# Attention by feature maps, then a cosine layer: queries in one wide step, key maxima as two float32r parts, a new order

## The chip, the cores and the metric

The kernel runs on one core of one Trainium2 chip. The core has TensorE (PE, matrix products into PSUM banks), VectorE (DVE), ScalarE (ACT), GpSimd (POOL) and SyncE (SP, which issues the DMAs). The metric is the time of one execution on the device, in microseconds (us). Line numbers (L574 and the like) are lines of the kernel before.

## The reference

```
phi(x):  proj = x @ w_phi                              # (576, 64) @ (64, 128)
         proj = proj - max(abs(proj), axis=-1)
         return concat(exp(proj), exp(-proj))          # 256 features
q_p, k_p = phi(q), phi(k)
kv  = k_p.T @ v ;  z = sum of k_p over the tokens
out = (q_p @ kv) / (q_p @ z + 1e-6)                    # per batch and head
x   = out, heads side by side                          # (4608, 512)
h   = x @ w_in ;  g = h * cos(h) ;  result = g @ w_out # w_in (512, 2048), w_out (2048, 512)
```

q, k and v have 8 batches, 8 heads, 576 tokens and 64 columns, in float32. w_in and w_out are float64; the kernel gets their bits.

## The kernel before, in words

**Attention.** Two heads of a batch form a pair; there are 32 pairs (`attention(u)`). The two heads lie one above the other, 64 partitions each, so that two products with 64 rows run beside each other in PE's array. For the queries of a pair `q_mm` projects a half of the tokens, 288 columns, for both heads into two banks; `q_copy` brings each of the four results to SBUF on ACT, `q_red` reduces each on DVE to the greatest absolute value, `q_max` joins them, `q_spread` (POOL) copies them to all quarters of the partitions, `q_turn` (DVE) turns them back to the layout of the queries, `q_sub` (POOL, one for each head) subtracts and `exp_q` (ACT) makes both exponentials. For the keys `k_mm` projects four blocks of 128 tokens of each head with the tokens on the partitions and `k_end` the remaining 64 of both heads; `k_max` (DVE) takes the greatest absolute value of each token. In pairs 0 to 7 (`K_SUMS`) the subtraction is made by PE: `k_sub` adds the product of `minus` (a matrix with -1 on the diagonal) with the maxima, read 128 times over, into the same bank; in the other pairs DVE subtracts (L569). `exp_k` makes the exponentials, `kv_mm` the sums over tokens, `kv_out` copies them, `z_mm` and `n_mm` make denominator and numerator, `invert`, `spread`, `turn` and `times` the quotient.

**FFN.** Weights are turned from float64 bits into two float32r parts (`convert`, 16 slices, four of them partly on POOL). Nine chunks of 512 tokens are worked through in slices of 128 columns of w_in: `mm1` is 12 products, then ACT and DVE make h cos(h) and its two parts, and `mm2` (or four `one`) is 12 products.

**Order.** Every piece of work is a `Step` on an engine, numbered as it is made. `ORDER` is a written list of these numbers; each engine issues its steps in that order and waits at each for what it needs. `plan()` gives each PSUM bank to the next use in that order. The cost beside each `Step` is a number for the planner that made the list and has no part in the program that runs. A step with `port=True` reads and writes SBUF alone on DVE or POOL. A step takes its buffers (`take`) and the last user frees them.

Of the kernel before, what the change touches and what calls it, by code (L numbers as in the profile page):

```python
# [17 lines left out]
P = 128  # L18
TWO_PI = 6.283185307179586
PI_2 = 1.5707963267948966  # L20
CT = 512
# [4 lines left out]
def phi_attention_then_cos_ffn(ctx: ExitStack, tc: tile.TileContext, qT, kT, vS, vT, w_phi, w_in, w_out, out):  # L26
# [41 lines left out]
    class Step:  # L68
# [16 lines left out]
    SHAPE = dict(mm1="full", mm2="full", one="full", k_mm="upper", k_end="full", t_mm="upper", t_end="full", s_mm="full", k_sub="full", kv_mm="left", n_mm="left", z_mm="quarter", q_mm="upper")  # L85
    ORDER = [
# [196 lines left out]
    for j in range(2):  # L283
# [5 lines left out]
    DVE.memset(warm, 0.0)  # L289

    minus = const.tile([P, P], F32, name="minus")
    POOL.memset(minus, -1.0)
    POOL.affine_select(out=minus, in_=minus, pattern=[[-1, P]], compare_op=ALU.is_equal, fill=0.0, base=0,
                       channel_multiplier=1)

# [637 lines left out]
```

## Time and profile before

| | |
|---|---|
| median of 3 runs | 1083.51 us (1080.97 to 1084.04) |
| profiled execution | 1081.44 us, its span 1079.7 us |
| granted TensorE clock | 1.000 |
| PE, busy in the span | 1069.3 us, 7678 products |
| DVE | 711.8 us, 1203 instructions |
| ACT | 720.8 us, 1388 instructions |
| POOL | 157.6 us, 187 instructions |
| DMA | 160.72 MB, mean 149 GB/s |

The span runs from the first to the last instruction of the profiled execution. A float32 product stands as two records of PE, a float32r product as one. Products overlap, so the time that one costs in a row of them is the distance from start to start. "Idle before" and what stands behind an arrow say how long an engine stood before an instruction and what it waited for.

### The profile page before, as it was taken

To read this page: it belongs to the slowest core of one execution; us is meant where nothing else is said; L and a number is where in the kernel's file an instruction comes from. 1 tells how busy PE (TensorE), PEld (TensorE's weight loads), DVE (VectorE), ACT (ScalarE), POOL (GpSimd) and SP (SyncE) were. 2 spreads that over 40 slices of the span, in tenths; PEclk is the share of its full clock that TensorE was granted. 3 is DMA by queue.
4 is the path that set the end of the run, shared out by engine and by line. 5 is a ranking of instruction groups with operands and counts; after the bars stand their busy time and mean duration, and the time that the engine had idled before them with its cause. 6 is when DMAs were issued, how large, how long until landed. Compare 5 with 4: busy or idle time off the path is not lost.

```text
span 1079.7 us, 19604 instructions
## 1 busy us (share of the span) xinstructions
PE 1069.3 (99%) x7678; PEld 830.6 (77%) x7678; DVE 711.8 (66%) x1203; ACT 720.8 (67%) x1388; POOL 157.6 (15%) x187
## 2 busy tenths in 40 slices
PE   9999999999999999999999999999999999999998
PEld 6666677787888887788677787786877878888886
DVE  6899999988898877645667456764564353434333
ACT  7888898878666669754785766757556654544443
POOL 5664322000000310101121011120120000000000
PEclk9999999999999999999999999999999999999999
DMA  7535644667655544275242643163231720540541
GB/s 217 154 119 189 180 132 143 209 202 249 235 167 191 210 153 153 105 242 185 63 123 73 243 148 107 56 232 135 75 87 47 277 90 1 187 174 10 185 157 49
DMA packets 92604, 160.72 MB, mean 149 GB/s; under 512 B 43744, under 2 KB 52064, under 8 KB 84320
## 3 DMA queue, kind: packets, MB, share of 16 engines
q1 hardware_dynamic: 92352, 159.41, 44.3%
q8 instruction: 60, 0.98, 0.4%
q14 instruction: 32, 0.26, 0.1%
q10 hardware_dynamic: 160, 0.07, 0.0%
HBM read 117.51 MB, written 41.94 MB: 148 GB/s over the span
## 4 chain that ended last, share of the span: by engine, by line
PE 87%; DVE 5%; issue 0%; DMA 0%; POOL 0%; ACT 0%; DVEq 0%; POOLq 0%
PE bank L782 36%; PE bank L816 12%; PE bank L818 12%; PE bank L817 12%; PE bank L675 4%; PE bank L626 4%; PE bank L665 2%; PE bank L434 2%; PE bank L476 2%; PE bank L632 1%; PE bank L552 1%; DMA out<-o_last 0%; DVE g_c__1300 L793 0%; DVE g_c__1130 L800 0%; DVE m_u__1584 L445 0%
## 5 line engine op out<-in xcount | busy, mean ns | idle before, releaser
L797 ACT ACT_TABLE_LOAD x23 | 29.5, 1283 | 0.4
L459 POOL COPY m_u__4056<-m_u__4056 32x36 f32<-32x36 f32 x3 | 1.6, 540 | 174.4 <-DVE m_u__4056 L454 174.3
L582 ACT ACT_TABLE_LOAD x15 | 19.2, 1283 | 0.8 <-DVE pk_u__2466 L569 0.5
L856 DVE TENSOR_TENSOR o<-bank,o 128x512 f32<-128x512 f32 x24 | 16.1, 678 | 0.1
L863 ACT ACTIVATE o<-bank 128x512 f32<-128x512 f32 x16 | 9.5, 592 | 5.5 <-PE bank L818 5.5
L782 PE MATMUL bank<-xh_c__6319,w 128*128 128x512 f32 x32 | 12.9, 402 | 0.0
L865 DVE COPY o<-bank 128x512 f32<-128x512 f32 x16 | 10.8, 674 | 3.1 <-PE bank L818 3.1
L782 PE MATMUL bank<-xh_c__5560,w 128*128 128x512 f32 x32 | 12.7, 398 | 0.0
L782 PE MATMUL bank<-xh_c__7588,w 128*128 128x512 f32 x32 | 12.7, 396 | 0.0
L782 PE MATMUL bank<-xh_c__4428,w 128*128 128x512 f32 x32 | 12.6, 393 | 0.0
L782 PE MATMUL bank<-xh_c__6921,w 128*128 128x512 f32 x32 | 12.5, 391 | 0.0
L782 PE MATMUL bank<-xh_c__6769,w 128*128 128x512 f32 x32 | 12.5, 390 | 0.0
L782 PE MATMUL bank<-xh_c__5807,w 128*128 128x512 f32 x32 | 12.5, 390 | 0.0
L782 PE MATMUL bank<-xh_c__7130,w 128*128 128x512 f32 x32 | 12.5, 390 | 0.0
L782 PE MATMUL bank<-xh_c__5878,w 128*128 128x512 f32 x32 | 12.5, 390 | 0.0
L782 PE MATMUL bank<-xh_c__7977,w 128*128 128x512 f32 x32 | 12.5, 390 | 0.0
L782 PE MATMUL bank<-xh_c__5928,w 128*128 128x512 f32 x32 | 12.5, 390 | 0.0
L782 PE MATMUL bank<-xh_c__8059,w 128*128 128x512 f32 x32 | 12.5, 390 | 0.0
L782 PE MATMUL bank<-xh_c__4632,w 128*128 128x512 f32 x32 | 12.5, 389 | 0.0
L782 PE MATMUL bank<-xh_c__8100,w 128*128 128x512 f32 x32 | 12.5, 389 | 0.0
L782 PE MATMUL bank<-xh_c__4557,w 128*128 128x512 f32 x32 | 12.5, 389 | 0.0
L782 PE MATMUL bank<-xh_c__4759,w 128*128 128x512 f32 x32 | 12.4, 389 | 0.0
(3872 smaller groups left out, 4075.7 us busy)
## 6 DMA issues: line engine op xcount, KB each, us to landing
w<-w_parts SPq DMA_DIRECT2D x48, 1024.0 KB, 5.3
w_parts<-w SPq DMA_DIRECT2D x16, 1024.0 KB, 5.7
vmain<-vS SPq DMA_DIRECT2D x32, 256.0 KB, 3.9
out<-o SPq DMA_DIRECT2D x32, 256.0 KB, 3.5
sums<-o SPq DMA_DIRECT2D x24, 256.0 KB, 3.3
o<-sums SPq DMA_DIRECT2D x24, 256.0 KB, 3.2
vtail<-vT SPq DMA_DIRECT2D x64, 16.0 KB, 3.4
out<-o_last SPq DMA_DIRECT2D x4, 256.0 KB, 2.0
```

What stands on the lines that cost most here:

```text
L434: PE.matmul(out=ps[j], lhsT=wphi[r, :], rhs=d["qr"][r, hf * HALF:(hf + 1) * HALF], start=True, stop=True)
L476: PE.matmul(out=ps[j][:, P * s:P * s + P], lhsT=x[r, P * s:P * s + P], rhs=wphi[r, :], start=(s == 0), stop=w, skip_group_check=True)
L582: ACT.activation(out=e[:, :, s * P:(s + 1) * P], in_=pk, func=AF.Exp, scale=1.0 - 2.0 * s)
L626: PE.matmul(out=acc[c:c + 64, n, i, :], lhsT=e[:, s, P * n + c:P * n + c + 64], rhs=vmain[u % 2][:, s, i, :], start=(s == 0 and i == 0 and ...
L665: PE.matmul(out=ps[32 * g:32 * g + 32], lhsT=d["z"][:, 2 * n + j, :], rhs=d["eq", j][:, n, hf * HALF:(hf + 1) * HALF], start=(n == 0), sto ...
L675: PE.matmul(out=d["nps", hf][64 * j:64 * j + 64], lhsT=d["kv"][:, 2 * n + j, :], rhs=d["eq", j][:, n, cut[hf]], start=(n == 0 and hf == 0) ...
L782: PE.matmul(out=h, lhsT=a[:, cs], rhs=d[b, kt], start=(k == 0), stop=(k == 3 * KT - 1))
L797: ACT.activation(out=m["g"], in_=m["g"], func=AF.Sin, bias=halfpi, scale=1.0)
L816: PE.matmul(out=a, lhsT=gh[:, t], rhs=w[:, 0], start=first, stop=False)
L817: PE.matmul(out=a, lhsT=gh[:, t], rhs=w[:, 1], start=False, stop=False)
L818: PE.matmul(out=a, lhsT=gl[:, t], rhs=w[:, 0], start=False, stop=last)
L856: DVE.tensor_tensor(out=o, in0=bank(acc[tb]), in1=o, op=ALU.add)
```

## The change

Queries: `q_mm` now projects 512 tokens of both heads in one step (two products with 512 columns), and a new step `q_end` projects the last 64 of both heads in one product with 128 columns over all 128 rows, from a block that is laid out on the host as the keys' already is. ACT copies two results of 512 columns and one of both ends; `q_red` reduces 576 columns of a head in one instruction. Keys of pairs 0 to 7: DVE splits each maximum into a float32r number and the float32r rest (`k_parts`, two instructions), and `k_sub` adds two float32r products in place of one in float32; `minus` is rounded to float32r once. `ORDER` is a new list, of 2848 steps instead of 2920. Code that no pair used (`Q_SUMS`, `t_mm`, `t_max`, `s_mm`, `s_exp`) is gone.

```diff
-    minus = const.tile([P, P], F32, name="minus")
+    minus_f = const.tile([P, P], F32, name="minus_f")
...
+    minus = const.tile([P, P], F32R, name="minus")
+    hi_of(POOL, minus, minus_f)
...
-            d["qr"] = new("qr", [P, S + P], F32, f"qr_u{u}_")
+            d["qr"] = new("qr", [P, (NSLOT + 1) * P], F32, f"qr_u{u}_")
-            SP.dma_start(out=d["qr"][:, 0:S + P if u in Q_SUMS else S], in_=qT[u][:, 0:S + P if u in Q_SUMS else S])
+            SP.dma_start(out=d["qr"], in_=qT[u])
...
-        def q_mm(hf):
+        def q_mm():
             for j in range(2):
                 r = slice(64 * j, 64 * j + 64)
-                PE.matmul(out=ps[j], lhsT=wphi[r, :], rhs=d["qr"][r, hf * HALF:(hf + 1) * HALF], start=True, stop=True)
+                PE.matmul(out=bank(qb[j]), lhsT=wphi[r, :], rhs=d["qr"][r, 0:CT], start=True, stop=True)
+        def q_end():
+            PE.matmul(out=bank(qb[2])[:, 0:P], lhsT=wphi, rhs=d["qr"][:, CT:CT + P], start=True, stop=True)
...
+            if i < 2:
+                ACT.activation(out=pq[:, i, 0:CT], in_=bank(qb[i]), func=AF.Copy, scale=1.0)
+            else:
+                ACT.activation(out=pq[:, :, CT:S], in_=bank(qb[2])[:, 0:P].rearrange("p (j s) -> p j s", j=2), func=AF.Copy,
+                               scale=1.0)
+        def q_red(j):
+            DVE.tensor_reduce(out=d["m1"][:, 2 * j * NJ:2 * (j + 1) * NJ],
+                              in_=d["pq"][:, j * S:(j + 1) * S].rearrange("p (j t) -> p j t", t=32), axis=AX.X,
                               op=ALU.max, apply_absolute_value=True, apply_transpose=True)
...
+        mm = Step("PE", 0.86, q_mm, [ld], take=qb[:2] + [b["pq"]], use=[b["qr"]], kind=phase + "q_mm")
+        me = Step("PE", 0.14, q_end, [ld], take=qb[2:], use=[b["qr"]], kind=phase + "q_end")
...
+        reds = [Step("DVE", 0.66, lambda j=j: q_red(j), [cps[j], cps[2]], use=[b["pq"]], kind=phase + "q_red")
+                for j in range(2)]
...
+        def k_parts(i):
+            tag = "pk" if i < 2 else "pk_t"
+            m = d["mk", i]
+            p = d["mp", i] = new(tag, [P, 2, NSLOT if i < 2 else 1], F32R, f"mp_u{u}_", "mp" + tag)
+            hi_of(DVE, p[:, 0], m)
+            lo_of(DVE, p[:, 1], m, p[:, 0])
         def k_sub(i):
...
-            PE.matmul(out=pv, lhsT=minus, rhs=d["mk", i].unsqueeze(2).broadcast_to([P, n, P]), start=False, stop=True,
-                      skip_group_check=True)
+            for r in range(2):
+                PE.matmul(out=pv, lhsT=minus, rhs=d["mp", i][:, r].unsqueeze(2).broadcast_to([P, n, P]), start=False,
+                          stop=(r == 1), skip_group_check=True)
...
-                kms[i] = Step("PE", 0.86 if i < 2 else 0.22, lambda i=i: k_sub(i), [kms[i]], use=[kb[i], pks[i]], kind="a.k_sub")
+                kms[i] = Step("DVE", 0.24, lambda i=i: k_parts(i), [kms[i]], use=[pks[i]], port=True, kind="a.k_parts")
+                kms[i] = Step("PE", 0.46 if i < 2 else 0.14, lambda i=i: k_sub(i), [kms[i]], use=[kb[i], pks[i]], kind="a.k_sub")
```

More of the change, by code (lines that the diff above doesn't have):

```diff
@@ L84, in phi_attention_then_cos_ffn @@
     SWITCH = dict(e=1.3, s=1.3, full=0.23, left=0.147, quarter=0.138, upper=0.195)
-    SHAPE = dict(mm1="full", mm2="full", one="full", k_mm="upper", k_end="full", t_mm="upper", t_end="full", s_mm="full", k_sub="full", kv_mm="left", n_mm="left", z_mm="quarter", q_mm="upper")
+    SHAPE = dict(mm1="full", mm2="full", one="full", k_mm="upper", k_end="full", q_end="full", k_sub="full", kv_mm="left", n_mm="left", z_mm="quarter", q_mm="upper")
     ORDER = [
[152 rows of a table removed]
[148 rows of a table added]
     ]
@@ L289, in phi_attention_then_cos_ffn @@
     DVE.memset(warm, 0.0)
-    minus = const.tile([P, P], F32, name="minus")
-    POOL.memset(minus, -1.0)
-    POOL.affine_select(out=minus, in_=minus, pattern=[[-1, P]], compare_op=ALU.is_equal, fill=0.0, base=0,
+    minus_f = const.tile([P, P], F32, name="minus_f")
+    POOL.memset(minus_f, -1.0)
+    POOL.affine_select(out=minus_f, in_=minus_f, pattern=[[-1, P]], compare_op=ALU.is_equal, fill=0.0, base=0,
                        channel_multiplier=1)
+    minus = const.tile([P, P], F32R, name="minus")
+    hi_of(POOL, minus, minus_f)
     vmain = [const.tile([P, NSLOT, 2, 65], F32, name=f"vmain{i}") for i in range(2)]
@@ L309, in phi_attention_then_cos_ffn @@
     Q_DVE = range(0)
-    Q_SUMS = range(0)
     K_SUMS = range(8)
@@ L427, in attention, with q_copy @@
         chain_v[u] = lv
-        def q_mm(hf):
-            d["qps", hf] = ps = [bank(d["qb", hf, j])[:, 0:HALF] for j in range(2)]
+        def q_mm():
             for j in range(2):
                 r = slice(64 * j, 64 * j + 64)
-                PE.matmul(out=ps[j], lhsT=wphi[r, :], rhs=d["qr"][r, hf * HALF:(hf + 1) * HALF], start=True, stop=True)
-        def q_copy(hf, j):
-            if (hf, j) == (0, 0):
+                PE.matmul(out=bank(qb[j]), lhsT=wphi[r, :], rhs=d["qr"][r, 0:CT], start=True, stop=True)
+        def q_end():
+            PE.matmul(out=bank(qb[2])[:, 0:P], lhsT=wphi, rhs=d["qr"][:, CT:CT + P], start=True, stop=True)
+        def q_copy(i):
+            if i == 0:
                 d["m1"] = new("pq", [P, 4 * NJ], F32, f"m1_u{u}_", "m1")
                 d["pq"] = new("pq", [P, 2 * S], F32, f"pq_u{u}_")
-            c = slice(j * S + hf * HALF, j * S + (hf + 1) * HALF)
-            ACT.activation(out=d["pq"][:, c], in_=d["qps", hf][j], func=AF.Copy, scale=1.0)
-        def q_red(hf, j):
-            c = slice(j * S + hf * HALF, j * S + (hf + 1) * HALF)
-            DVE.tensor_reduce(out=d["m1"][:, (2 * j + hf) * NJ:(2 * j + hf + 1) * NJ],
-                              in_=d["pq"][:, c].rearrange("p (j t) -> p j t", t=32), axis=AX.X,
+            pq = d["pq"].rearrange("p (j s) -> p j s", j=2)
+            if i < 2:
[6 more added lines that the diff above has]
+                              in_=d["pq"][:, j * S:(j + 1) * S].rearrange("p (j t) -> p j t", t=32), axis=AX.X,
                               op=ALU.max, apply_absolute_value=True, apply_transpose=True)
@@ L477, in project @@
                               start=(s == 0), stop=w, skip_group_check=True)
-        def t_mm():
-            project([bank(qb[j]) for j in range(2)], d["qr"], True)
-        def t_end():
-            PE.matmul(out=bank(qb[2])[:, 0:P], lhsT=d["qr"][:, S:S + P], rhs=wphi, start=True, stop=True)
-        def t_max(i):
-            n = NSLOT if i < 2 else 1
-            if i == 0:
-                d["mq"] = new("pq", [P, 4 * NJ], F32, f"m1_u{u}_", "m1")
-            DVE.tensor_reduce(out=d["mq"][:, NSLOT * i:NSLOT * i + n],
-                              in_=bank(qb[i])[:, 0:P * n].rearrange("p (g f) -> p g f", f=P), axis=AX.X, op=ALU.max,
-                              apply_absolute_value=True)
@@ L493, in s_mm @@
-        def s_mm():
-            ps = [bank(sb_[i]) for i in range(3)]
-            for j in range(2):
-                r = slice(64 * j, 64 * j + 64)
-                PE.matmul(out=ps[j], lhsT=wphi[r, :], rhs=d["qr"][r, 0:CT], start=True, stop=False, skip_group_check=True)
-            PE.matmul(out=ps[2][:, 0:P], lhsT=wphi, rhs=d["qr"][:, S:S + P], start=True, stop=False, skip_group_check=True)
-            for i in range(3):
-                n = NSLOT if i < 2 else 1
-                for s in range(n):
-                    c = NSLOT * i + s
-                    PE.matmul(out=ps[i][:, P * s:P * s + P], lhsT=d["mq"][:, c:c + 1].broadcast_to([P, P]), rhs=minus,
-                              start=False, stop=True, skip_group_check=True)
@@ L506, in s_exp @@
-        def s_exp(j):
-            e = d["eq", j] = new("eq", [P, 2, S], F32, f"eq_u{u}_")
-            for s in range(2):
-                ACT.activation(out=e[:, s, 0:CT], in_=bank(sb_[j]), func=AF.Exp, scale=1.0 - 2.0 * s)
-            for s in range(2):
-                ACT.activation(out=e[:, s, CT:S], in_=bank(sb_[2])[:, 64 * j:64 * j + 64], func=AF.Exp, scale=1.0 - 2.0 * s)
-        eqs, eqb = [], []
-        if u in Q_SUMS:
-            qb = [Buf("bank", "a") for _ in range(3)]
-            sb_ = [Buf("bank", "a") for _ in range(3)]
-            tm = Step("PE", 0.88, t_mm, [ld], take=qb[:2] + [b["pq"]], use=[b["qr"]], kind="a.t_mm")
-            te = Step("PE", 0.22, t_end, [ld], take=qb[2:], use=[b["qr"]], kind="a.t_end")
-            tr = None
-            reds = []
-            for i in range(3):
-                tr = Step("DVE", 0.67 if i < 2 else 0.28, lambda i=i: t_max(i), [te if i == 2 else tm, tr], use=[qb[i], b["pq"]],
-                          kind="a.t_max")
-                reds.append(tr)
-            sm = Step("PE", 3.4, s_mm, reds, take=sb_, use=[b["qr"], b["pq"]], kind="a.s_mm")
-            qs = [sm]
-        else:
-            reds, mm = [], None
-            for hf in range(2):
-                pair = [Buf("bank", "a"), Buf("bank", "a")]
-                d["qb", hf, 0], d["qb", hf, 1] = pair
-                mm = Step("PE", 0.49, lambda hf=hf: q_mm(hf), [ld, mm], take=pair + ([] if hf else [b["pq"]]),
-                          use=[b["qr"]] + ([b["pq"]] if hf else []), kind=phase + "q_mm")
-                for j in range(2):
-                    cp = Step("ACT", 0.3, lambda hf=hf, j=j: q_copy(hf, j), [mm] + reds[:1], use=[pair[j], b["pq"]],
-                              kind=phase + "q_copy")
-                    reds.append(cp)
-            cps, reds = reds, []
-            for i, cp in enumerate(cps):
-                reds.append(Step("DVE", 0.37, lambda i=i: q_red(i // 2, i % 2), [cp], use=[b["pq"]], kind=phase + "q_red"))
-            qm = Step("DVE", 0.41, q_max, reds, take=[b["bq"]], use=[b["pq"]], port=True, kind=phase + "q_max")
-            qm = Step("POOL", 0.45, q_spread, [qm], use=[b["bq"]], port=True, kind=phase + "q_spread")
-            qm = Step("DVE", 1.3, q_turn, [qm], use=[b["bq"]], kind=phase + "q_turn")
-            qs = [Step(qname, qcost, lambda j=j: q_sub(j), [qm], use=[b["pq"], b["bq"]], port=True, kind=phase + "q_sub") for j in range(2)]
@@ new lines, in attention @@
+        eqs, eqb = [], []
+        qb = [Buf("bank", "a") for _ in range(3)]
+        mm = Step("PE", 0.86, q_mm, [ld], take=qb[:2] + [b["pq"]], use=[b["qr"]], kind=phase + "q_mm")
+        me = Step("PE", 0.14, q_end, [ld], take=qb[2:], use=[b["qr"]], kind=phase + "q_end")
+        cps = []
+        for i in range(3):
+            cps.append(Step("ACT", 0.52 if i < 2 else 0.2, lambda i=i: q_copy(i), [me if i == 2 else mm] + cps[:1], use=[qb[i], b["pq"]],
+                            kind=phase + "q_copy"))
@@ new lines, in attention @@
+        reds = [Step("DVE", 0.66, lambda j=j: q_red(j), [cps[j], cps[2]], use=[b["pq"]], kind=phase + "q_red")
+                for j in range(2)]
+        qm = Step("DVE", 0.41, q_max, reds, take=[b["bq"]], use=[b["pq"]], port=True, kind=phase + "q_max")
+        qm = Step("POOL", 0.45, q_spread, [qm], use=[b["bq"]], port=True, kind=phase + "q_spread")
+        qm = Step("DVE", 1.3, q_turn, [qm], use=[b["bq"]], kind=phase + "q_turn")
+        qs = [Step(qname, qcost, lambda j=j: q_sub(j), [qm], use=[b["pq"], b["bq"]], port=True, kind=phase + "q_sub") for j in range(2)]
@@ L564, in k_max @@
             DVE.tensor_reduce(out=m, in_=pv, axis=AX.X, op=ALU.max, apply_absolute_value=True)
-            d["mk", i] = m
             if u in K_SUMS:
+                d["mk", i] = m
                 return
@@ L600, in attention @@
             if u in K_SUMS:
-                kms[i] = Step("PE", 0.86 if i < 2 else 0.22, lambda i=i: k_sub(i), [kms[i]], use=[kb[i], pks[i]], kind="a.k_sub")
-        gate = [] if early or u in Q_SUMS or u in K_SUMS else kms + qs
+                kms[i] = Step("DVE", 0.24, lambda i=i: k_parts(i), [kms[i]], use=[pks[i]], port=True, kind="a.k_parts")
+                kms[i] = Step("PE", 0.46 if i < 2 else 0.14, lambda i=i: k_sub(i), [kms[i]], use=[kb[i], pks[i]], kind="a.k_sub")
+        gate = [] if early or u in K_SUMS else kms + qs
         eks, ekb = [], []
@@ L610, in attention @@
             e = Buf("eq")
-            eqs.append(Step("ACT", 1.15 if u not in Q_SUMS else 1.75, lambda j=j: (s_exp if u in Q_SUMS else exp_q)(j),
-                            ([sm] if u in Q_SUMS else [qs[j]]) + gate, take=[e], use=[sb_[j], sb_[2]] if u in Q_SUMS else [b["pq"]],
+            eqs.append(Step("ACT", 1.15, lambda j=j: exp_q(j),
+                            [qs[j]] + gate, take=[e], use=[b["pq"]],
                             table="e", kind=phase + "exp_q"))
@@ L898, in _arrange, with blocks @@
     m = S - n * P
-    def blocks(x, w):
+    def blocks(x):
+        w = n * P
         xp = x.reshape(NU, 2, S, D).transpose(0, 1, 3, 2)
@@ L908, in blocks @@
         return xT.reshape(NU, 2 * D, w + P)
-    qT, kT = blocks(q, S), blocks(k, n * P)
+    qT, kT = blocks(q), blocks(k)
     vp = v.reshape(NU, 2, S, D)
```

300 rows, old and new, of the table ORDER are left out of this document.

## The prediction

> **What bounds the kernel now.** I read the page's engine shares first, then the busy time by stages, then what TensorE (PE) waited for, and then the timeline of PE and VectorE (DVE) in the first 110 us, where all steps of the change on keys lie.
>
> ```profile
> span 1079.7 us, 19604 instructions
> ...
> PE 1069.3 (99%) x7678; PEld 830.6 (77%) x7678; DVE 711.8 (66%) x1203; ACT 720.8 (67%) x1388; POOL 157.6 (15%) x187
> ```
>
> ```profile
> 0.00:27.00 27.00, 24.89 (x298) 18.03 (x300) 17.29 (x36) 20.08 (x45) 15.58 (x28) 1.00 0.74 217
> 27.00:54.00 27.00, 26.32 (x339) 16.73 (x340) 22.86 (x43) 23.14 (x57) 16.42 (x17) 1.00 0.50 154
> 54.00:108.00 54.00, 51.24 (x559) 35.02 (x552) 51.79 (x82) 45.52 (x96) 30.24 (x28) 1.00 0.48 154
> 108.00:216.00 108.00, 107.58 (x1112) 77.95 (x1111) 103.89 (x191) 97.68 (x205) 24.77 (x32) 1.00 0.53 166
> ```
>
> ```profile
> PE bank L574 <- DVE mk_u__945 L564: 0.8, 1, 0.8
> PE bank L574 <- DVE mk_u__915 L564: 0.8, 1, 0.8
> ...
> PE bank L574 <- DVE mk_u__938 L564: 0.7, 1, 0.7
> PE bank L574 <- DVE mk_u__750 L564: 0.7, 1, 0.7
> ```
>
> The columns behind each stage's length are PE, PE's weight loads, DVE, ScalarE (ACT), GpSimd (POOL). Over the whole span PE is the bound: after 108 us it is practically never idle, so there each us of PE work is a us of time. But the share of 66% for DVE is an average over two regimes. From 54 to 108 us DVE is busy 51.79 of 54 us, as much as PE, and PE's own waits there are for the maxima of keys that DVE makes (line 564). Setting each PE step's start-to-start time beside its undisturbed repeats, PE waits 6.6 us in all after its first product, all but 0.2 of it before 133 us. So the start is bound by PE and DVE together, the rest by PE alone.
>
> **The change on PE.** Times between starts are the prices, since matmuls overlap.
>
> ```profile
> 10.00 1.03 PE L574 MATMUL bank<-mk_u__164,minus 128*128 128x512 f32 x2
> 10.86 0.38 PE L552 MATMUL bank<-wphi,kr_u__131 128*128 128x128 f32 x2
> 11.08 0.39 PE L574 MATMUL bank<-mk_u__178,minus 128*128 128x128 f32 x2
> ...
> 42.97 1.24 PE L434 MATMUL bank<-qr_u__454,wphi 64*128 64x288 f32 x8
> 44.04 1.06 PE L476 MATMUL bank<-wphi,kr_u__630 64*128 64x128 f32 x16
> ...
> 46.85 0.59 PE L675 MATMUL bank<-eq_u__613,kv_u__625 128*64 128x512 f32 x1
> ...
> 47.28 0.59 PE L675 MATMUL bank<-eq_u__613,kv_u__625 128*64 128x512 f32 x1
> ...
> 299.70 0.39 PE L816 MATMUL bank<-w,gh_c__3496 128*128 128x512 f32 x1
> ...
> 302.42 0.39 PE L816 MATMUL bank<-w,gh_c__3527 128*128 128x512 f32 x1
> ```
>
> Subtraction of key maxima: a float32 matmul of 512 columns is two records and takes 10.86 - 10.00 = 0.86 us; one of 128 columns takes 11.08 - 10.86 = 0.22. In float32r twelve matmuls of 512 columns take 302.42 - 299.70 = 2.72, so 0.227 each. The two parts cost 0.45 in place of 0.86 for 16 steps: -6.5 us. No float32r matmul of 128 columns is in the trace: two of them lie between 0.11 (a quarter of 0.45) and 0.22 (the float32 row); I take 0.14, nearer to the row of the same format, for 8 steps: -0.7 us (ends -0.9 and 0). Together -7.2 us.
>
> [...]
>
> Queries: the two halves of 288 columns take 44.04 - 42.97 = 1.07, of which 0.10 is the change of array shape in front; 0.97 is the price. A float32 pass of 512 columns takes 47.28 - 46.85 = 0.43, so the pair step of 512 tokens costs 0.86, and the short step is the same shape as the keys' end, 0.22 (the cost written beside the step is 0.14). That is 1.08 for 0.97, in 32 pairs: +3.5 us. The short step uses the whole array, so it also sits at a change of shape. Pricing every change of shape or format as the trace repeats it (about 0.05 us between a float32 step of the whole array and a float32r one, 0.15 to 0.28 for the others), and counting them along the two written-out orders of PE steps, gives 37.2 us before and 38.6 after: +1.4 (ends 0, if the search has hidden them, and +3, if each short step pays a full change). PE's sum is -7.2 + 3.5 + 1.4 = **-2.3 us**.
>
> **The change on DVE.**
>
> ```profile
> 6.77 0.69 DVE L564 TENSOR_REDUCE mk_u__162<-bank 128x4 f32<-128x512 f32 x1 [5.69 <-PE bank L476]
> ...
> 8.29 1.56 DVE L445 TRANSPOSE_TENSOR_REDUCE m_u__146<-pq_u__147 128x9 f32<-128x288 f32 x4 [0.23 <-ACT pq_u__147 L441]
> 9.88 0.19 DVE L453 TENSOR_TENSOR m_u__170<-m_u__146 64x36 f32<-64x36 f32 x1
> 10.11 0.18 DVE L454 TENSOR_TENSOR m_u__171<-m_u__170 32x36 f32<-32x36 f32 x1
> ...
> 15.98 0.69 DVE L355 TENSOR_SCALAR w_t_f__247<-w_t_f__247 128x1024 uint32<-128x1024 uint32 x1
> 16.70 1.22 DVE L357 SCALAR_TENSOR_TENSOR w_t_f__248<-w_raw_f__244,w_t_f__247 128x1024 uint32<-128x1024 uint32 x1
> ```
>
> Each pair of parts (`k_parts`) is two small instructions, the second reading what the first wrote. Two such in a row start 10.11 - 9.88 = 0.23 apart and the last holds the engine some 0.13 more: 0.36 a step (the cost written beside it is 0.24), 24 steps, all in the first 72 us of PE work: +8.6 us. The reductions of queries take (9.88 - 8.29)/4 = 0.40 for 288 columns, so about 0.10 fixed and 0.30 for the columns, and 0.70 for 576: 1.40 instead of 1.60 a pair. Now I count along the orders what stands ahead of the point where PE has done 101 us of its own work. Now: 29 key maxima, 40 reductions of queries, 10 maxima and 9 turns of queries, 4 weights' bit steps, 8 inversions, 18 products and the rest come to 87.6 us at start-to-start prices. After: 24 parts (+8.6), 20 reductions at 0.70 for 40 at 0.40 (-2.0), and by the new order one more bit step (0.7 + 1.2 + 0.7), two more small steps and one turn less, together +3.1: 97.3 us. PE's k_sub saving is made in the same stretch, so DVE gets 10 us more to do within the same PE time.
>
> What DVE loses now, besides work:
>
> ```profile
> DVE mk_u__435 L564 <- PE bank L476: 1.2, 1, 1.2
> ...
> DVE bq_u__486 L463 <- POOL m_u__480 L459: 0.9, 1, 0.9
> ...
> DVE m_u__146 L445 <- ACT pq_u__147 L441: 0.2, 1, 0.2
> ```
>
> ```profile
> 32.49 1.18 DVE L683 TENSOR_SCALAR dn_u__490<-dn_u__490 128x9 f32<-128x9 f32 x1
> ```
>
> ```profile
> 32.24 2.77 POOL L467 TENSOR_TENSOR pq_u__380<-pq_u__380,bq_u__486 128x576 f32<-128x576 f32 x2 [1.56 <-DVE bq_u__486 L463]
> ```
>
> ```profile
> L683 DVE TENSOR_SCALAR dn_u__1476<-dn_u__1476 x1: 173/173/173, 112.4 to 112.4; 128x9 f32<-128x9 f32 x1
> ```
>
> ```profile
> 77.72 2.34 DVE L454 TENSOR_TENSOR m_u__1100<-m_u__1099 32x36 f32<-32x36 f32 x1
> ...
> 99.47 1.67 DVE L793 SCALAR_TENSOR_TENSOR g_c__1300<-g_c__1300,hs_c__1299 128x512 f32<-128x512 int32 x1
> ```
>
> After its first maximum DVE waits nine times up to 132 us, from 1.2 down to 0.2: 7.4 us. And an SBUF instruction of DVE that starts while POOL works stands until POOL's instruction ends: 1.18 us at 32.49 under POOL's subtraction of 32.24, against 0.173 alone. Fourteen such before 102 us, the last at 99.47, add 14.4 us.
>
> Balance now: DVE's start 6.8 + 87.6 + 7.4 + 14.4 = 116.2 against PE's start 5.1 + 101 = 106.1. The difference of 10.1 is 4.0 more than the 6.1 us that PE has waited by then: so much lead DVE's results have on their readers. After: 6.8 + 97.3 + idle + stalls - 106.1 - 4.0 = -6.0 + idle + stalls. In the new order right behind all of the first five turns of queries, the moment at which POOL starts its two subtractions of 1.4 us, stand SBUF instructions of DVE: parts twice, inversions twice, a bit step (now behind four of them). So stalls of 14 to 17 us are my value, nearest to what the same places cost now, and idle about 3 (DVE's queue is fuller). PE's waits become 11 to 14, I take 12.8: +6.2 us over now. The ends: all of the idle time gone and a third of the stalls (waits 4), or idle as now and 20 us of stalls (waits 21).
>
> **Costed at nothing.**
>
> ```profile
> 7.25 1.32 ACT L441 ACTIVATE pq_u__147<-bank 128x288 f32<-128x288 f32 x4 [3.93 <-PE bank L434]
> 8.42 1.51 ACT L441 ACTIVATE pq_u__157<-bank 128x288 f32<-128x288 f32 x4
> ...
> 10.44 0.72 POOL L459 COPY m_u__171<-m_u__171 32x36 f32<-32x36 f32 x3 [8.22 <-DVE m_u__171 L454]
> ```
>
> Copies of queries: 4 at (8.42 - 7.25)/4 = 0.29 against two of 0.48 and one of about 0.17, 1.13 for 1.16. POOL's rounding of `minus` fits into its 8.22 us of idle time ahead of 10.44; were it late, the first subtraction at 8.8 us would wait. Queries load 64 columns of padding more, 32 KB a pair, from SP's queue whose loads run ahead; only the first pair's keys, issued behind them, could come some 0.1 us later.
>
> **The sum.** Profiled execution: span 1079.7, time 1081.4, so 1.7 lies around the span. 1081.4 - 2.3 + 6.2 = 1085.3. The median of the three runs, 1083.5, stands 2.1 above that execution; on it I forecast 1087.4.
>
> **Rivals.** (a) DVE's lead absorbs the parts and PE waits as now: only PE's sum counts, 1083.5 - 2.3 = 1081.2, no measurable change. For it: DVE's waits at 27 to 54 us show idle time to be filled; against: 54 to 108 us has only 2.2 us unfilled. (b) Faster: the new order puts DVE's SBUF instructions where POOL rests and what DVE loses falls from 21.8 to about 10.5: PE's waits 4.5, time 1083.5 - 2.3 - 2.1 = 1079.1. It decides from waits under 5.7, so a loss under 11.7. For it: that the stalls are many and of 1 us each; against: the turns above. (c) Most of the 24 parts meet POOL, which is busy 30.24 of 54 us: 8 us more of stalls, waits 21, time 1095.6. [...] (d) The float32r products could run at the float32 price, then the 7.2 us are missing: 1083.5 + 4.9 + 6.2 = 1094.6; the FFN's rows at 0.227 speak against it.
>
> **How the numbers follow.** About 0.3%, 3.25 us, is what a measurement of this kernel can tell from no change. My forecast (waits 9 to 17, times 1083.5 to 1091.5) has 0.50, of which 0.15 lies within 0.3%; (a) 0.25; (b) 0.15; (c) and (d) 0.10. So faster 0.15, same 0.40, slower 0.45. The range of 8 in 10 reaches from (b)'s 1079.5 into (c), 1094; the forecast's own is 1083.5 to 1091.5.
>
> **What would show it.** PE's records of the keys' subtraction start 0.227 apart and number 2 of 0.22 to 0.23 instead of 0.43; queries 0.86 and 0.22. The stage from 0 to 108 us should show DVE busier than now with fewer waits on PE, ACT or POOL, PE less busy, and PE's list of waits longer and headed by the parts. From 216 us on nothing but PE's sum should differ. Wrong would make me: stalled DVE instructions under ten before 108 us, or PE ahead of DVE by more than 4 us.

## The result and the profile after

The changed kernel took 1096.37 us (median of four runs, 1095.67 to 1097.60) against 1083.48 for the kernel before beside it: a ratio of 1.0134, interval 1.0122 to 1.0147, with 12.9 us between the medians. The runs of the kernel before lie at 1081.0 and at 1083.5 to 1084.0, so a difference of about 1 us between two medians says little. The profiled execution took 1096.01 us. The forecast had the direction (1087.4) and not the size: the result lies above its range, which ended at 1094.

Engine shares of the profile after, then its stages (columns as before: PE, PE's weight loads, DVE, ACT, GpSimd (POOL), granted clock, DMA share, GB/s), then the longest of PE's waits:

```profile
span 1094.3 us, 19390 instructions
...
PE 1072.8 (98%) x7614; PEld 829.8 (76%) x7614; DVE 719.3 (66%) x1187; ACT 719.1 (66%) x1356; POOL 161.3 (15%) x188
```

```profile
0.00:27.00 27.00, 23.19 (x276) 16.55 (x276) 19.31 (x41) 18.62 (x41) 13.80 (x28) 1.00 0.74 215
27.00:54.00 27.00, 22.35 (x284) 15.79 (x286) 24.51 (x49) 17.95 (x40) 14.71 (x13) 0.87 0.43 133
54.00:108.00 54.00, 48.19 (x480) 31.20 (x478) 51.30 (x90) 42.05 (x89) 34.23 (x27) 0.94 0.47 144
108.00:216.00 108.00, 105.32 (x1100) 75.29 (x1096) 102.96 (x174) 96.71 (x199) 30.86 (x37) 1.00 0.53 165
```

```profile
PE bank L430 <- DVE rb_u__1197 L657: 2.5, 1, 2.5
PE bank L632 <- DVE rb_u__1449 L657: 2.2, 1, 2.2
PE bank L530 <- DVE mp_u__435 L51: 2.1, 1, 2.1
PE bank L530 <- DVE mp_u__435 L54: 1.8, 1, 1.8
PE bank L530 <- DVE mp_u__825 L51: 1.8, 1, 1.8
PE bank L530 <- DVE mp_u__976 L54: 1.5, 1, 1.5
```

All of the loss lies ahead of 135 us. From 27 to 54 us PE is busy 22.35 us where it was 26.32, and PE's list of waits, whose longest entry behind its first product was 0.8, now begins at 2.5. Four of these six are for the new parts (`mp_u`, lines 51 and 54 of the helpers that `k_parts` calls); the two longest end with a step of a quotient (`rb_u`, line 657). The granted clock, 1.00 in these stages before, is 0.87 and 0.94: the records show half clock from 28.98 to 35.80, 59.70 to 63.11 and 93.83 to 97.24 us, each less than 1 us behind the end of a wait of PE of 1.8 to 2.5 us (28.71, 59.53 and 92.99). The wait of 2.2 us, which ended at 125.72, brought none.

The cause of such a wait is seen where DVE's timeline (first fence) is laid on GpSimd's (second fence) and PE's (third); columns are start, duration, engine, line:

```profile
26.21 2.19 DVE L51 TENSOR_SCALAR mp_u__432<-mk_u__314 128x4 fp32r<-128x4 f32 x1
28.43 0.16 DVE L54 TENSOR_TENSOR mp_u__432<-mk_u__314,mp_u__432 128x4 fp32r<-128x4 f32 x1
28.51 0.15 DVE L51 TENSOR_SCALAR mp_u__435<-mk_u__430 128x1 fp32r<-128x1 f32 x1
28.69 2.12 DVE L54 TENSOR_TENSOR mp_u__435<-mk_u__430,mp_u__435 128x1 fp32r<-128x1 f32 x1
...
57.21 2.19 DVE L54 TENSOR_TENSOR mp_u__822<-mk_u__820,mp_u__822 128x4 fp32r<-128x4 f32 x1
...
89.13 2.85 DVE L750 SCALAR_TENSOR_TENSOR g_c__1168<-g_c__1168,hs_c__1167 128x512 f32<-128x512 int32 x1
91.91 0.77 DVE L653 STREAM_TRANSPOSE rb_u__1197<-d_u__1129 128x576 f32<-128x576 f32 x1
92.71 0.82 DVE L657 TENSOR_TENSOR rb_u__1197<-bank,rb_u__1197 128x64 f32<-128x64 f32 x2
```

```profile
26.03 2.33 POOL L54 TENSOR_TENSOR w_t_f__258<-w_t_f__258,w 128x1024 f32<-128x1024 f32 x1
28.45 2.35 POOL L369 TENSOR_TENSOR w<-w_t_f__258,w_t_f__259 128x1024 fp32r<-128x1024 f32 x1
...
57.00 2.38 POOL L369 TENSOR_TENSOR w<-w_t_f__504,w_t_f__505 128x1024 fp32r<-128x1024 f32 x1
```

```profile
28.71 0.32 PE L530 MATMUL bank<-mp_u__435,minus 128*128 128x128 f32 x1 [2.08 <-DVE mp_u__435 L51]
30.87 0.48 PE L530 MATMUL bank<-mp_u__435,minus 128*128 128x128 f32 x1 [1.83 <-DVE mp_u__435 L54]
31.14 1.17 PE L530 MATMUL bank<-mp_u__432,minus 128*128 128x512 f32 x2
...
39.42 0.68 PE L530 MATMUL bank<-mp_u__519,minus 128*128 128x512 f32 x2
```

Three of these instructions, 0.16 us elsewhere, take 2.1 to 2.2: an instruction of GpSimd of 2.3 to 2.4 us has begun 0.2 us ahead of each, and they end when that ends (26.21 + 2.19 = 28.40 against 26.03 + 2.33 = 28.36). I call that a hold. Both parts of one maximum were held in a row here, by two steps of a weight on GpSimd, and PE stood 3.9 us at one short subtraction. The longest wait has the same cause at one remove: an FFN instruction at 89.13, 0.68 us alone, stood 2.85 under GpSimd's step on a weight from 89.08 to 91.43, and the quotient behind it came late. Before 135 us 23 instructions of DVE were held, for 25.7 us (16 and 15.8 before); 8 of the 48 instructions of parts took 11.1 us of that.

An account of DVE makes kernels comparable. It is taken at the moment when PE has done 101 us of its own work at undisturbed prices: DVE's first maximum, plus its work, what it lost held (each instruction over its usual duration), and its idle gaps. The four add up to the moment by construction: the account says where the time went, and the experiments must say why.

```
kernel               first   work   held (count)   idle    moment
before                 6.8   80.9   14.4 (14)      12.9    115.0
after                  6.7   89.1   25.7 (23)       9.1    130.6
after - before        -0.1   +8.2  +11.3           -3.8    +15.6
```

By 160 us PE has lost 16.3 us more beyond its own work than in the kernel before, and nothing more is lost; PE's sum of step prices is 2.35 us less and its first product starts 0.4 later, which comes near to the 14.6 by which the span has grown.

### The profile page after: what moved, and what is told of

The parts are those of the page before. It is cut to its first block, busy times and chain, and to the rows that moved or that the text cites. A ratio compares the mean times of both kernels' runs of the same rounds, so it can differ in the third digit from the quotient of the medians.

```text
span 1094.3 us, 19390 instructions
## 1 busy us (share of the span) xinstructions
PE 1072.8 (98%) x7614; PEld 829.8 (76%) x7614; DVE 719.3 (66%) x1187; ACT 719.1 (66%) x1356; POOL 161.3 (15%) x188
## 4 chain that ended last, share of the span: by engine, by line
PE 90%; DVE 8%; DMA 1%; issue 1%; POOL 0%; SPq 0%; ACT 0%; DVEq 0%; POOLq 0%
PE bank L739 35%; PE bank L773 12%; PE bank L775 12%; PE bank L774 12%; PE bank L632 5%; PE bank L583 4%; PE bank L622 3%; PE bank L476 2%; PE bank L430 2%; PE bank L589 1%; PE bank L433 1%; PE bank L500 1%; DMA qr_u__135<-qT 0%; PE bank L530 0%; DVE g_c__1168 L750 0%
## 5 line engine op out<-in xcount | busy, mean ns | idle before, releaser
L739 PE MATMUL bank<-xh_c__5222,w 128*128 128x512 f32 x32 | 12.8, 400 | 0.0
L739 PE MATMUL bank<-xh_c__7676,w 128*128 128x512 f32 x32 | 12.8, 399 | 0.0
```

The lines of the kernel that those rows point to most:

```text
L739: PE.matmul(out=h, lhsT=a[:, cs], rhs=d[b, kt], start=(k == 0), stop=(k == 3 * KT - 1))
```

## The experiments

**Which part of the change loses.** Theory 1: DVE's parts, through their work and by standing behind GpSimd. Theory 2: the new order. Four kernels separate queries, products, parts and order.

e1, the changed kernel without parts: the maxima are reduced straight into float32r (so k_sub subtracts the rounded maximum) and the second product is of a zero constant.

```
-            m = new(tag, [P, n], F32, ...)
+            m = new(tag, [P, n], F32R if u in K_SUMS else F32, ...)
...                                   # k_parts: no instruction
-                PE.matmul(out=pv, lhsT=minus, rhs=d["mp", i][:, r]...
+                PE.matmul(out=pv, lhsT=minus, rhs=(none[:, 0:n] if r else d["mk", i])...
```

> The changed kernel and its order, but the maxima of keys are reduced straight into float32r and the second part is a constant zero: PE does the same products, VectorE has none of the 48 small instructions of the parts (the rests of the maxima are left out of the result). Theory 1 (the parts on VectorE: about 8 us of work and 11.1 us of standing behind GpSimd, which hold PE up and let its clock fall): PE's waits fall from 18 to at most 7, the granted clock is 1.0 throughout, time 1077 to 1083 us. Theory 2 (the new order itself puts too much in front of the keys on VectorE, with or without parts): time stays above 1090 us.

1083.34 us, ratio 1.0001 (0.9991 to 1.0010). Without parts the change costs nothing; it gains nothing either, 0.3 us above the range of theory 1, and PE still has one stretch at half clock (106.1 to 109.5 us). DVE's holds before 135 us are about 20 us (20 instructions), 6 less than in the changed kernel and not the 11.1 that the parts lost: some of what comes in their place is held itself.

e2, the changed kernel with its queries and order, but keys subtracted in one float32 product as before.

> The changed kernel and its order, but keys as before: one float32 product for each subtraction and no parts. Against e1_one_part only PE's 24 subtractions differ, by 7.2 us at the rows' prices. Theory 1: PE's waits stay near those of the kernel before, time 1083.5 - 2.3 + 7.2 = 1088 us, down to 1084 if the longer products fill waits. Theory 2: above 1095 us.

1086.39 us, ratio 1.0040 (1.0027 to 1.0053). So by the medians, each step uncertain by 1 to 2 us, queries and order cost 3.3 us, the float32r products give back 3.1 (e1 below e2), and the parts cost 13.0 (after above e1).

e3, the kernel before in its own order, with parts made right behind each maximum and float32r products.

> The kernel before and its order, with the keys' part of the change alone: the two parts are made right behind each maximum, PE subtracts with two float32r products. Theory 1: VectorE gets 8 us of work and further stalls into the stretch it shares with PE; PE saves 7.2 us and waits 12 to 20 us more, time 1089 to 1097 us. Theory 2 (parts do no harm in an order that is not the new one): 1083.5 - 7.2 = 1076 us.

1099.40 us, ratio 1.0154 (1.0135 to 1.0174): the change on keys, in an order made for the kernel before, loses at least as much as the whole change (the intervals overlap), and more than the 1089 to 1097 of theory 1.

e4, all of the change, its steps put into the order of before.

> All of the change, but each step at the place that it, or the step it replaces, has in the order before (the parts right behind their maximum). Theory 1: as slow as the changed kernel or nearly so, 1089 to 1100 us. Theory 2: PE's sum alone, about 1081 us.

1104.72 us, ratio 1.0200 (1.0184 to 1.0216). Theory 2, which put this run at 1081, falls: the new order wins back 8 us of what the steps lose in the old one. The time is 5 us over the range of theory 1.

**What the products save.** e5: before's order and queries, no parts, two float32r products (the maximum rounded, as in e1, and a zero constant). e6: the first of these products alone.

```
-            PE.matmul(out=pv, lhsT=minus, rhs=d["mk", i]...        # float32
+            for r in range(2):                                     # e5; e6 has r = 0 alone
+                PE.matmul(out=pv, lhsT=minus, rhs=(none[:, 0:n] if r else d["mk", i])...   # float32r
```

> The kernel before, in its own order, with its queries. The maxima of keys are reduced straight into float32r (so they are rounded to that format, and the subtraction is not exact), no parts are made, and k_sub adds two float32r products, the second of a constant zero. DVE's work is that of before; PE has the products of the change. Theory (what the change lost is DVE's parts, and behind them PE's waits; the products themselves save 7.2 us): PE's sum falls by 7.2, its waits grow by at most 3, as DVE becomes the bound of the start a little sooner: 1076 to 1080 us, ratio 0.993 to 0.997. Rival (the float32r products or their changes of format cost PE what they save, or DVE already sets the end of the start, so that a shorter PE only waits): within 0.2% of before, 1081.5 to 1085.

> As the run with two products, but k_sub has the one product of the rounded maximum alone: PE saves 16 x 0.227 and 8 x 0.07 us more, 4.2 us. If PE bounds the start: 4.2 us under the run with two products, 1072 to 1076 us. If DVE bounds it (rival): less than 1.5 us under that run.

e5: 1080.89 us, ratio 0.9981 (0.9972 to 0.9991). e6: 1080.28, ratio 0.9975 (0.9965 to 0.9984). I had expected 1076 to 1080 and 1072 to 1076. PE's sum of step prices falls by 7.3 and 11.5 us, and what PE loses beyond it rises from 7.2 to 14.7 and 17.6: three quarters and more of a saving on PE in the start turn into waits and, for 6.8 us from 64.4 and from 63.8, into products at half clock. That fits a start whose end DVE sets already before the change.

**What GpSimd's work does.** e7 is the changed kernel without GpSimd's subtraction on queries in pairs 0 to 7 and without two of its steps on its own weights; e9 leaves the same out of the kernel before.

```
         def rest():
+            if name == "POOL":
+                return
...                                   # low() likewise
         def q_sub(j):
-            qeng.tensor_tensor(...)
+            if u >= 8:
+                qeng.tensor_tensor(...)
```

> The changed kernel with its order and its parts, but GpSimd leaves out its subtraction on queries in pairs 0 to 7 and the rounding and rest of its own weights (the output lacks these). DVE's instruction list is as in the changed kernel. Theory of the stalls (the parts' own work of 8 to 9 us is half the loss, DVE standing behind GpSimd's instructions the other half, 25.7 us of stalls in the changed kernel): stalls fall below 10 us, PE's waits from 18 to 6 or less and the half-clock stretches go: 1080 to 1088 us. Rival (the parts' work and the tight order bind, stalls lie beside other waits): 1092 us or more.

> The kernel before, with the same work left out on GpSimd as in the run e7 (its subtraction on queries in pairs 0 to 7, the rounding and rest of its own weights; the output lacks these). It is the control for e7, which took 1076.7 us. Theory (DVE's own work on the parts is covered once nothing holds DVE; only standing behind GpSimd costs): stalls fall from 15.8 to about 4 us, PE's waits from 6.6 to 2 or less, then PE bounds all the way, and the parts' kernel keeps its PE sum of -2.3 us: 1077 to 1080 us, at or above e7. Rival (the parts' 8 us of DVE work cost time of their own, and e7 was fast because GpSimd's results were missing): 1074 us or less, 3 us and more under e7.

e7: 1076.74 us, ratio 0.9941 (0.9926 to 0.9956). e9: 1076.49, ratio 0.9946 (0.9929 to 0.9963). Both are under their ranges. Stages of e7 (first two rows) and e9 (last two):

```profile
27.00:54.00 27.00, 27.00 (x398) 18.57 (x396) 25.23 (x64) 25.67 (x58) 4.67 (x10) 1.00 0.54 165
54.00:108.00 54.00, 51.71 (x531) 34.57 (x530) 51.33 (x93) 49.39 (x99) 14.55 (x16) 1.00 0.51 161
```

```profile
27.00:54.00 27.00, 27.00 (x344) 17.56 (x344) 21.18 (x46) 24.17 (x59) 3.95 (x9) 1.00 0.50 155
54.00:108.00 54.00, 54.00 (x594) 36.65 (x591) 48.65 (x94) 49.81 (x106) 10.78 (x18) 1.00 0.53 165
```

In e7 five instructions are held for 6.0 us, and PE is busy all of 27 to 54 us: 19.7 us less of holds, 19.3 us less of span. That is not the price of the holds alone, as GpSimd's results also come sooner; the comparison that counts is with e9, where the same is left out. In e9 DVE has 18.0 us idle by the moment of the account: with few holds the parts' 7 us of work fit into DVE's idle time, and the two kernels take the same time. PE's gain of 2.3 us does not show in e7: it loses 5.0 us beyond its sum, e9 2.8.

**The half clock.** e8 adds three groups of eight products: in PE's two waits at the short subtraction of pair 2, and behind the short subtraction of pair 6 (they write into the bank of the short keys of these pairs and touch the accumulation there, so these values are not the reference's; my expectation overlooked that).

```
+            def fill(n):
+                for _ in range(n):
+                    PE.matmul(out=d["kps", 2][:, 2 * P:3 * P], lhsT=warm, rhs=warm, start=True, stop=True, ...)
             for r in range(2):
+                if u == 2 and i == 2:
+                    fill(8)
...
+            if u == 6 and i == 2:
+                fill(8)
```

> The changed kernel with 24 products of 128 columns (each two records) added on PE into spare columns of a bank, 8 in front of and 8 behind the short k_sub of pair 2 and 8 behind that of pair 6, where PE stands longest before 60 us. They compute nothing that is read. Theory (the half clock behind these waits adds to the time: 6.8 + 3.4 us at half speed, 5.1 us lost): the granted clock from 27 to 63 us rises to 1.0 and the time falls by 2 to 5 us, 1091.5 to 1094.5. Rival (DVE sets the end of this stretch, so that a slow PE only uses up what it would wait): within 1 us of the changed kernel, 1095.5 to 1097.5, or slower by the filled time of up to 5 us.

1097.67 us, ratio 1.0132 (1.0117 to 1.0147), the same as the changed kernel's 1.0134. The first two groups did their work on the clock: the stage from 27 to 54 us, 0.87 in the changed kernel, is at 1.00. The third did not fill a wait: it starts at 74.97, when pair 6's wait of 1.49 us is over, and takes PE 3.2 us at half clock. Half clock is left from 60.8 and from 74.4 us, 3.4 us each.

```profile
27.00:54.00 27.00, 25.13 (x322) 18.24 (x320) 25.87 (x51) 19.49 (x44) 16.20 (x14) 1.00 0.48 146
```

```profile
32.42 0.32 PE L535 MATMUL bank<-mp_u__435,minus 128*128 128x128 f32 x1
...
39.47 0.68 PE L535 MATMUL bank<-mp_u__535,minus 128*128 128x512 f32 x2
```

From that short subtraction to the next pair's, e8 takes 39.47 - 32.42 = 7.05 us, the changed kernel 39.42 - 30.87 = 8.55: with PE at full clock this stretch is 1.5 us shorter. But this profile of e8 was 1.5 us late already at 21 us, ahead of any fill, so from 36 to 73 us it is only level with the changed kernel (within 0.2 us). Right behind the third group it is 3.3 us late, and from 129 us on 1.7. So the time of e8 holds a gain from the clock and the cost of a misplaced group at once and can't price either: the theory's 2 to 5 us are neither shown nor refuted, and what the half clock costs is open.

**DVE's work against its holds.** e10 is the changed kernel with the subtraction on queries of pairs 0 to 7 on DVE; e11 is e6 with the same.

```
-    Q_DVE = range(0)
+    Q_DVE = range(8)
```

> The changed kernel, all of its computation, with the subtraction on queries of pairs 0 to 7 made by DVE at the places of the same order, in place of GpSimd. DVE gets 16 instructions of about 0.7 us more (11 us); what it stands behind GpSimd falls from 25.7 to 8 us or less (GpSimd's weights and spreads are left). Theory of the stalls: -17.7 + 11 is 6 to 7 us less than the changed kernel, 1088 to 1092 us. Rival (DVE's work counts for more than its stalls, which lie beside other waits): 1097 us or more.

> The run e6 (before's order and queries, maxima of keys rounded to float32r, one product) with the subtraction on queries of pairs 0 to 7 on DVE. Stalls fall from 14.6 to 4 us or less, work grows by 11 us: if both count alike, 1079 to 1082 us, no change from e6 (1080.3); if stalls count for more, as waits of PE come in lumps, 1076 to 1078 us; if work counts for more, 1084 us or more.

e10: 1100.04 us, ratio 1.0170 (1.0152 to 1.0187). e11: 1089.74, ratio 1.0069 (1.0049 to 1.0088). Both expectations missed, for one reason: the moved subtractions read SBUF too, and are held by GpSimd's weights. DVE and GpSimd in e10 (two subtractions of 0.75 take 4.31), and PE's wait behind it:

```profile
50.99 4.31 DVE L469 TENSOR_TENSOR pq_u__497<-pq_u__497,bq_u__744 128x576 f32<-128x576 f32 x2
```

```profile
49.52 2.35 POOL L54 TENSOR_TENSOR w_t_f__504<-w_t_f__504,w 128x1024 f32<-128x1024 f32 x1
51.95 2.73 POOL L369 TENSOR_TENSOR w<-w_t_f__504,w_t_f__505 128x1024 fp32r<-128x1024 f32 x1
```

```profile
PE bank L632 <- DVE dn_u__748 L638: 4.2, 1, 4.2
```

Holds fell to 14.3 us, not to 8; work rose by 13.2. The account closes: -11.4 + 13.2 + 0.8 of idle time - 0.1 = 2.5 us later than the changed kernel, whose span is 2.5 us shorter than e10's. In e11, up to the moment of the account, work rises by 12.1 us and holds fall by 0.7.

**Which instructions are held.** e12 is the changed kernel, each pair of parts made by three reductions; e13 is the kernel before without DVE's addition of 1e-6 to the denominators, its most often held instruction; e14 is e6 without it.

```
-            hi_of(DVE, p[:, 0], m)
-            lo_of(DVE, p[:, 1], m, p[:, 0])
+            DVE.tensor_reduce(out=p[:, 0], in_=m[:, 0].unsqueeze(2), axis=AX.X, op=ALU.max, negate=True)
+            DVE.tensor_reduce(out=m[:, 1], in_=p[:, 0].bitcast(F32).unsqueeze(2), axis=AX.X, op=ALU.max)
+            DVE.tensor_reduce(out=p[:, 1], in_=m.rearrange("p r n -> p n r"), axis=AX.X, op=ALU.add, negate=True)
...                                   # minus holds +1
-            DVE.tensor_scalar(out=dn, in0=dn, scalar1=1e-6, scalar2=None, op0=ALU.add)      # e13, e14
```

> The changed kernel, all of its computation and its order, with each pair of parts made by three small reductions of DVE in place of one scalar and one tensor instruction: the maximum rounded and negated, its copy beside the maximum, and the negated sum of the two; k_sub then adds with a plain identity. Reductions that read SBUF run at their usual 0.43 to 0.48 us inside GpSimd's instructions in the traces; the parts' two instructions lost 11.1 us behind them. Theory (the kind of instruction decides what is held): none of the parts' reductions is held, stalls fall from 25.7 to about 15, DVE's own work grows by 24 x 0.1 to 0.15 = 3 us: 7 to 8 us less than the changed kernel, 1087 to 1091 us. Rival (any small SBUF instruction of DVE is held, or the next instruction takes over the hold): 1095 us or more.

> The kernel before, without DVE's addition of 1e-6 to the denominators in every pair (the output lacks that addition). This scalar instruction is 8 of the 16 that stood behind GpSimd, 6.9 of 15.8 us. Theory: the reciprocal behind it is not held, stalls fall to 9 us, DVE's work by 1.5 us, PE's waits from 6.6 to about 2, where PE bounds the start: 1077 to 1080 us. Rival (the reciprocal is held in its place): 1081.5 to 1084 us.

> The run e6 (before's order and queries, the maxima of keys rounded to float32r by the reduction and one product for the subtraction; 1080.3 us), without the addition of 1e-6. DVE sets the end of the start there with 14.6 us of stalls. Theory: 7 us of stalls and 1.5 us of work less on DVE come off the time nearly one for one: 1072 to 1075 us. Rival (the reciprocal is held): 1079 to 1081 us.

e12: 1089.86 us, ratio 1.0068 (1.0050 to 1.0086), 6.5 us under the changed kernel with all of its computation. Its parts on DVE, and GpSimd's instruction over them:

```profile
29.40 0.13 DVE L527 TENSOR_REDUCE mp_u__462<-mk_u__456 128x1 fp32r<-128x1 f32 x1
29.57 0.15 DVE L528 TENSOR_REDUCE mk_u__456<-mp_u__462 128x1 f32<-128x1 f32 x1
29.76 0.15 DVE L530 TENSOR_REDUCE mp_u__462<-mk_u__456 128x1 fp32r<-128x2 f32 x1
29.94 1.65 DVE L455 TENSOR_TENSOR m_u__518<-m_u__343 64x36 f32<-64x36 f32 x1
```

```profile
29.18 2.36 POOL L369 TENSOR_TENSOR w<-w_t_f__262,w_t_f__263 128x1024 fp32r<-128x1024 f32 x1
```

Three reductions pass under GpSimd's instruction at 0.13 to 0.15 us; the next tensor operation, with the same instruction over it, stands till it ends (31.59 against 31.54). So the kind decides. These rows alone would not show it for the first part, since the changed kernel's scalar instruction on one column passes too (28.51 above, 0.15 us under GpSimd's of 28.45); the reductions of four columns do: 20 of them start in e12 under a tensor instruction of GpSimd that runs on for 0.4 us or more, and take 0.14 to 0.16 us, where the scalar and tensor instructions on four columns took up to 2.19. Some of the hold passes on to what comes next: held time falls by 8.8 us to 16.9, not by the parts' 11.1, and DVE's work grows by 3.4.

e13: 1079.91 us, ratio 0.9972 (0.9961 to 0.9984). e14: 1078.27, ratio 0.9959 (0.9944 to 0.9974). Rows of e13, DVE and then GpSimd:

```profile
86.56 0.27 DVE L684 RECIPROCAL d_u__1180<-dn_u__1178 128x18 f32<-128x18 f32 x1
86.75 1.45 DVE L799 TENSOR_TENSOR g_c__1125<-hs_c__1124,g_c__1125 128x512 f32<-128x512 f32 x1
```

```profile
86.24 3.24 POOL L467 TENSOR_TENSOR pq_u__982<-pq_u__982,bq_u__1176 128x576 f32<-128x576 f32 x2
```

The reciprocal takes its usual 0.27 us under GpSimd's subtraction and the tensor operation behind it is held (1.45 us for 0.69). Held time up to 135 us falls from 15.8 to 10.3, 2.9 us come off the time. e14 was to fall by 5 to 8 us and fell by 2.0: its DVE has 16.5 us of idle time at the moment of the account, so I take it that DVE's work no longer sets the end there. e14 beats both kernels; it gives up the maximum's rest and the 1e-6.

## Why the prediction missed

**PE's sum: right.** Step prices along the two orders give 1062.07 before and 1059.72 after, -2.35 for a forecast of -2.3. One price was off with little effect on the sum. The float32r product of 512 columns starts 0.216 behind the one ahead in the changed kernel, for a forecast of 0.227. The short one, which I put at 0.07 (0.14 for two), is in these rows of e5:

```profile
27.73 0.28 PE L581 MATMUL bank<-none,minus 128*128 128x128 f32 x1
27.84 0.28 PE L581 MATMUL bank<-mk_u__421,minus 128*128 128x128 f32 x1
27.95 0.28 PE L581 MATMUL bank<-none,minus 128*128 128x128 f32 x1
28.06 0.43 PE L581 MATMUL bank<-mk_u__449,minus 128*128 128x512 f32 x1
```

They start 0.11 apart, two at 0.22, no cheaper than the 0.22 of one in float32 (behind a product of 512 columns the first gap is 0.06, and two take 0.17).

**DVE's work and idle time: right.** Forecast +9.7 of work and 4.4 less of idle time; measured +8.2 and 3.8 less. The reduction of 576 columns, put at 0.70, takes (10.20 - 8.73)/2 = 0.735 in the profile after.

**What DVE stands behind GpSimd: the term that failed.** The prediction took "stalls of 14 to 17 us", with 20 as the end of the range. Measured: 25.7. The miss of 9 to 12 us is the miss of the time (1096.4 against 1087.4). The step at fault is the list of places. It looked for DVE's instructions "right behind all of the first five turns of queries", where GpSimd starts its subtractions of 1.4 us, and left out GpSimd's steps on weights, 2.3 to 2.4 us each. Four of the eight held instructions of parts stood behind these (26.21, 28.69 and 57.21 above, and one at 72.85), for 7.6 of their 11.1 us. It also priced the new instructions by what such places cost before, though 48 were new and GpSimd is busy for 30 of the 54 us from 54 to 108. (That share taken as the chance of a hold would have overshot: 8 of the 48 were held.) e12 tests the term: with the parts as reductions holds fall by 8.8 us and the time by 6.5.

**PE's waits.** Forecast 12.8; measured 18, and 5.7 us more in products at half clock, which the prediction did not have. The list was to be headed by the parts; it is headed by two that end with a step of a quotient. On DVE's account little of that is a further cause: what a slow PE costs DVE would stand in its idle time, which is less than before; 1.8 us of it, at 34.4 and 37.4, are waits for PE. No run prices the half clock by itself.

**The rivals.** What happened is (c), to which (c) and (d) together gave 0.10: its 1095.6, from 8 us more of holds, lies 0.8 us from the result, and its argument, that GpSimd is busy for more than half of these 54 us, was the one to weigh. The nearness is in part luck: (c) had most of the 24 parts meet GpSimd for 8 us, while 7 of the 24 were held, for 11.1. It was kept out of the middle by a count over one kind of GpSimd's work. (a) and (d) fall: e1 shows that without the parts the time is that of before, and the products cost 0.216, not the float32 price. (b) fails for this order: holds rose. "Stalled DVE instructions under ten before 108 us" was named as what would prove me wrong; it went the other way.

## What to carry to other kernels

Where an engine is the second bound of a stage, cost a new instruction on it by what can hold it: lay its place in the order beside everything that the engine seen to hold it (GpSimd here) runs there, not beside one kind, and charge what is left of that other instruction. An instruction of 0.16 us took up to 2.2 here, and the waits behind it went straight to PE (1.5 to 2.1 us). Before moving work, look whether another kind of instruction gives the same result without being held: three reductions in place of two arithmetic instructions won back 6.5 of the 12.9 us lost.

## What the runs showed of the hardware

- Held behind GpSimd's tensor instructions: DVE's tensor operations with two inputs in SBUF (0.16 us become up to 2.1 on one column, 2.2 on four) and its scalar operations on four columns (0.16 become 2.2) and on nine (0.17 become 1.19, L683 at 98.06 in the kernel before). But at 41.49 in the changed kernel a scalar operation on 1024 columns took its usual 0.69 just behind the start of GpSimd's two subtractions (41.47), and these took 4.35 for 2.8. Not held: reductions from SBUF (0.13 to 0.16), the transposed reductions of queries in the kernel before (0.42 to 0.48; 0.45 each in the four from 8.29), the reciprocal (0.27), tensor operations that read one input from a bank (L569 of the kernel before: 0.69 at 84.28, where GpSimd's instruction has 1.65 us to run, and 0.69 elsewhere), and the scalar operation on one column (0.10 to 0.15 at 28.51, 54.02 and 72.69 in the changed kernel). I had expected any small instruction to be held, and the prediction's sentence that an SBUF instruction of DVE stands until POOL's ends is too wide.
- PE's clock was halved in the changed kernel (0.50 granted) for 6.82 us from 28.98 and for 3.41 from 59.70 and from 93.83, behind waits of 1.8 to 2.5 us. The length of one wait does not decide it: a wait of 2.4 us in e12 (it ended at 44.9) brought none, and in e6 half clock came at 63.8 amid waits of 0.8, 0.9 and 1.0 us. What decides is open. I had costed waits of PE once, without what can follow them.
- A reduction can write float32r directly, and k_sub takes it at 0.22 us a product (27.45 to 27.67 in e5).
